# A band buffer's clear moved behind four small GpSimd steps, and three one-input VectorE steps made two-input ones

## The chip, the cores and the metric

The kernel runs on one core of a Trainium2 chip. The metric is the device time of one execution in microseconds (us). The compute engines are TensorE (PE), VectorE (DVE), ScalarE (ACT) and GpSimd (POOL); SyncE (SP) issues most of the DMAs.

## The reference

Two unrelated layers on 2048 tokens of width 448, their outputs side by side:

```python
# A: attention over a dilated window: 16 heads of 28, each token sees itself and 7 tokens at distance 2, 4, .. 14
qkv = x @ wqkv
logits = einsum("bhsd,bhswd->bhsw", q, kg) * scale      # kg, vg: k and v gathered at pos - 2*w, masked below 0
o = einsum("bhsw,bhswd->bhsd", softmax(logits), vg)
a = o.reshape(B, S, D) @ wo
# B: a diagonal complex state space (S5)
dt = exp(log_dt); Lam_bar = exp(dt * Lam)
B_bar = ((Lam_bar - 1) / Lam)[:, None] * Bmat
h[t] = Lam_bar * h[t-1] + B_bar @ x[t]                   # a recurrence over 2048 tokens
y = 2 * real(Cmat @ h) + x * Dskip
return concatenate([a, y], -1)                           # bf16, 1 x 2048 x 896
```

## The kernel before

Nothing schedules the kernel but a string, ORDER. Each of its words names a small function (an "op") with digits for its arguments, a PSUM bank behind "@" and an engine for evictions ("." is ScalarE, "=" is VectorE). The words are worked off once, from left to right, and each engine then runs its own instructions in that order; semaphores alone tie the engines together. So a word that is moved changes the order only on the engines that it uses.

**Attention.** Tokens are transposed on TensorE (XI, XA, XH; their evictions are xi, xa, xh) or by DMA, q and k are made in 64-row blocks (QA, QS, QK) and evicted (qk, qh). The logits are products on VectorE (P, L417, one for each pair of window positions, 24 on 128x2048), summed over each head's rows by TensorE (E_, L429 and L433). They are brought to ScalarE (lt), transposed by DMA (TD, L451), and go through a softmax (sma, smb, smc; sma begins at L457). The weights are then laid out as a band: AL spreads them with matmuls, al evicts them into a buffer Ak (its first two parts are one tile, Ak0, which must be zero outside the band), ad writes Ak to DRAM and sp reads it back on a slant into PT, whose clears on GpSimd are L985. AV and W_ finish the attention.

**The state space.** 2048 steps are done in blocks of T = 4 with rotations. Before that, the parameters of the 448 states, held as 128 partitions by G = 7 columns, are worked out by small ops:

- PP, pcopy, pa, pb, pc bring in the parameters and their exponentials (VectorE and ScalarE). pb leaves f8, each state's angle for 2T tokens as a fraction of a turn.
- pe (VectorE, L639 to L642) makes u4, the angles for five distances, 128x35, and takes off the nearest whole number by adding and subtracting MAGIC = 1.5 * 2^23.
- pf (ScalarE, L646 to L648) takes sine and cosine of u4.
- pd_ (VectorE, L633 to L635) does the same rounding for f8, which gives fT; "way" is a column of -1 and 1.
- tk (L692 on ScalarE, L694 on VectorE), ty, tf and ts make tables of angles for 256 blocks from fT.
- pg (VectorE, L654 to L664) makes co, the correction factors for one to four tokens, and the columns c1t and c2t; rb (L715) spreads co into rotation matrices R.
- ab (GpSimd, L853, four instructions on 64x14) makes from co the columns acol and bcol, which are read by hp much later.

Two more words matter: mz clears Ak0 on GpSimd (L683), and OZ closes the first pools and clears a strip of Z3 on GpSimd (L961). B's input xnB is transposed by DMA into xbuf (xt, L746), which BU multiplies; L899 (xd) multiplies xnB with Dskip.

At the start, GpSimd makes constants (cols, kph, iota, masks), the last of which is shf. The column cols[:, 5:6] holds MAGIC. Around the parameters stand, in ORDER: `pe WF4 pf pd_ tk1= QA01 tk0. QA00 qk000. QA10 QS30 XH1 xh1. XA10 xa10. QA11`. QA11's last matmul (L386) reads what xh1 (a copy of 64x512 on ScalarE) evicts from XH1's bank (L339); its first three are L385.

The loads of all inputs stand first on SP's queue and run to some 30 us; most are issued without a wait for a compute engine.

Of the kernel before, what the change touches and what calls it, by code (L numbers as in the profile page):

```python
# [11 lines left out]
ALU = mybir.AluOpType  # L12
# [8 lines left out]
G = 7  # L21
# [6 lines left out]
MAGIC = 12582912.0  # L28
# [4 lines left out]
WU@0 XI0@1 xi00. LC PP@2 pcopy pa XI2@3 pb xi20. pc WF0 XI1@4 WF1 WF2 xi10= xi01= WF3 xi11= pe WF4 pf pd_ tk1= QA01@5  # L33
tk0. QA00 qk000. QA10@6 QS30@7 XH1@2 xh1. XA10@3 xa10. QA11 XA11@0 xa11. QS20@1 pg rb3 rb0 qk010. wj. QS01@4 ty1
QS11@5 QK041@23 ty0 QK061@06 qk011. QK060 qk001. qk030. qk020. P000 P001 tf0 qh001. qh011. qh000. xt1 ts00 QK040
qk041. QS21@5 QS31@4 P010 P011 P020 qk021. qk031. QK050@71 V_011@03 qk040. qh010. QK051 ts10 V_101@54 qk050. tk4.
E_00@26 P021 E_02 ts20 hc0 P030 E_01 V_010 v011. qk051. V_100 QK100@73 ty4 v010. ty5 P031 P040 tk5. QK101 qk100.
QK111@10 E_03 P041 P050 QK110 qk101. P051 tf2 P060 v100. QK130@73 mz ts02 qk110. v101. tk3. E_04 E_05 qk111. P061 E_06
ts12 tk2. ts22 QK141@51 QK131 qk131. qk130. lt00 QK121@40 QK120 qk120. ty2 BD0 QK140 QK150@37 lt01 TD0 qk121. qk140.
QK161@24 P100 P101 P110 P111 qk141. ci3. QK151 qk151. qk150. V_411@60 P120 P121 P130 ty3 E_10@53 E_12 QK160 qh110.  # L40
P131 P140 V_000@17 qh111. xt3 qh101. qh100. V_410 v410. v411. E_11 P141 P150 xt2 xt0 E_13 V_111@42 V_001 ci2. v000.
sma0 v001. hc1 V_511@60 P151 P160 LD P161 ci0= CD3 V_510 v510. V_500@17 V_110 V_501 tf1 v511. V_401@60 smb0 ci1. ab
E_14 smc0 E_15 E_16 lt10 lt11 v501. v110. tk6. CD2 v111. V_400 v401. dk. TD1 BU100@53 BU000@74 xd2 v400. CD0 BU001 BD1
CD1 BU101 BU111@20 AL1@6 sma1 OZ OP pm3 z00. z10. al1. ad1 AL0@7 BR01 BR11 z11= v500. al0. BU200@56 BU110 smb1 BR12
z01= ts01 smc1 BU301@17 BU201 BU011@34 BU010 z20= BU300 z12. z30= ts11 BR02 BR13 ca3 cs3 BR21 BU500@25 z02= BU501 ca6
ca1 xd0 z13. z21. BU211@13 BR03 z03. z50. BU210 BR22 ts21 xd1 UP1 y1. ad0 BR31 pm0 cs1 AL2@6 wo sp0 z22= UP0 y0. cs6
BR51 BR23 z51. pm1 sa0 BU400@21 pm4 z23. UP2 al2. sp1 AL3@0 AX@4 y2= BU310@56 BU311 z31. BU401 BU511@73 ca2 ca4 sb0
BR32 z32. BU510 ax= adx ad2 al3. BR33 sd0 DN1@4 BR52 cs4 cs2 DN0@5 dn0 z40. BR41 z33. UP3 y3= pm2 ad3 z52. sp2 ca5 dn1
sa2 z41. ty6 BU600@02 tf3 BR53 z53. BU411@75 BU601 AV000@6 AV030@4 av030. H_00@1 BU410 sb2 z60. BR61 h00 H_01@4 h01
ts03 av000. z61. UP5 y5. BR42 AV001@0 AV010@6 sd2 AV031@1 z42. av010. AV021@2 av021. AV020@3 AV011@4 av020= spx hp010  # L50
BR43 z43. av001. av031= BU610@76 UP4 DN2@2 av011. y4= ts13 ca0 DN3@3 dn3 BU611 BR62 z62. W_11@0 W_20@1 dn2 W_01@4
hp012 sa4 hp020 w20. ts23 sp3 w01. BR63 z63. cs5 sb4 H_03@5 h03 sw0 sd4 w11. W_10@3 W_00@2 H_02@7 ow01 W_21@1 w10.
ow10 hp011 UP6 y6= h02 W_31@4 AV130@5 w00. w21= ow20 ow00 av130. AV111@0 av111. AV100@3 AV120@2 AV110@6 av120. av110=
AV131@5 av131= av100. AV121@7 AV101@0 av121. ow11 ow21 sa6 W_30@1 DN5@2 W_60@6 DN4@3 sw2 av101. dn4 w30= sb6 W_71@7
w31. ow31 W_50@5 hp110 hp121 hp023 dn5 hp021 W_41@0 W_61@4 H_05@3 W_51@1 sd6 cs0 ow30 H_04@2 sw4 w71. hp120 w61= w51=
DN6@7 ow71 dn6 w50. C33@5 hy0 ow50 ow61 H_06@4 h05 w41. hp013 hz0 h04 ow41 ow51 C31@0 hp022 hp122 h06 hp111 hy1 hp124
hp025 sw6 hp115 hp112 C30@1 c30 hy2 c31 C32@7 c32 hp015 oc31 hp125 hy5 hp123 C03@3 hz1 W_40@2 hp024 hp113 hz5 hp014
W_70@4 hp114 hp016 hp126 oc30 hz2 hp026 hy4 hy3 hz4 hp116 hz3 hy6 oc32 hz6 w60. w40. w70. xd3 ow70 ow60 C00@1 c33
C01@0 c00 c01 C02@7 c02 C13@6 C11@2 C10@4 oc33 C12@5 c03 c10 c11 oc01 C21@1 C20@0 oc00 ow40 C22@7 CH0@3 oc10 oc03 oc02
CH1@4 c12 oc12 c13 c20 oc13 oc11 c21 c22 ch0 oc20 oc21 oc22 oh0 ch1 oh1  # L60
"""

@with_exitstack
def kernel(
# [17 lines left out]
    V = nc.vector  # L82
# [111 lines left out]
    cols = const.tile([128, 6], F32, tag="cols")  # L194
    hpib, phi, sg, way = (cols[:, i:i + 1] for i in range(4))
# [402 lines left out]
    def small(name, *shape):  # L598
        return const.tile([128, *shape], F32, tag=name, name=name)
    P3 = small("P3", 3, G)  # L600
    lre, lim, ld = (P3[:, i] for i in range(3))
    f8, rk, c1t, c2t, co, fT = (small(*a) for a in (("f8", G), ("rk", 5, G), ("c1t", G), ("c2t", G), ("co", T, 2, G), ("fT", G)))
    dt, are, km, u4, k4, sc2 = (small(*a) for a in (("dt", G), ("are", G), ("km", G), ("u4", 5, G), ("k4", 5, G), ("sc2", 2, 5, G)))
# [26 lines left out]

    @op
    def pd_():
        V.tensor_scalar(km[:], f8[:], MAGIC, None, ALU.add)  # L633
        V.scalar_tensor_tensor(fT[:], km[:], MAGIC, f8[:], ALU.subtract, ALU.subtract)
        V.tensor_scalar(fT[:], fT[:], way, None, ALU.mult)  # L635

    @op
    def pe():
        V.tensor_tensor(u4[:], f8[:].unsqueeze(1).to_broadcast((128, 5, G)), kph[:, 0], ALU.mult)  # L639
        V.tensor_tensor(u4[:], u4[:], kph[:, 1], ALU.add)  # L640
        V.tensor_scalar(k4[:], u4[:], MAGIC, None, ALU.add)  # L641
        V.scalar_tensor_tensor(u4[:], k4[:], MAGIC, u4[:], ALU.subtract, ALU.subtract)  # L642

    @op
# [383 lines left out]
```

## Time and profile before

| | before |
|---|---|
| median of 3 runs | 125.67 us (125.66 to 125.69) |
| the profiled execution's own time | 125.67 us |
| its span, first to last instruction | 124.0 us |
| granted TensorE clock | 1.00 |
| TensorE busy | 117.2 us, 95% of the span |
| VectorE busy | 114.0 us, 92% |
| ScalarE busy | 103.8 us, 84% |
| GpSimd busy | 22.7 us, 18% |

How to read it: a row of a timeline gives the start, the duration, the engine, the line, the operation, what is written and read with shapes, how many such instructions follow each other, and in brackets how long the engine sat idle before and who ended that. The chain that ended last is followed back from the last instruction, at each step to what released it; its rows give start, duration and what ran. "issue" in it is time in which nothing shown was waited for. The digits are the busy tenths in 40 equal slices of the span.

### The profile page before, as it was taken

The page shows a single profiled execution, that of the slowest core. Times are in us where ns is not written, and L with a number is a line of the kernel's source. Part 1 is how long each engine was busy: PE and PEld are TensorE (multiplying, and loading weights), DVE is VectorE, ACT ScalarE, POOL GpSimd, SP SyncE. Part 2 cuts the span into 40 slices and gives each one's busy share as a digit, 9 for nine tenths or more (in the row PEclk, how much of TensorE's full clock was granted, in tenths as well). Part 3 has the DMA queues.
Part 4 walks back from the last instruction along what each step waited for, and adds up shares of the span by engine and source line. Part 5 has one row for each costly group of instructions (what it writes and reads, how often), then busy time and mean ns, then how long its engine had stood idle before and what let it go on. Part 6 is the DMA issues. An engine that isn't in the chain of part 4 may idle for free.

```text
span 124.0 us, 2908 instructions
## 1 busy us (share of the span) xinstructions
PE 117.2 (95%) x1061; PEld 58.8 (47%) x1071; DVE 114.0 (92%) x207; ACT 103.8 (84%) x202; POOL 22.7 (18%) x49
## 2 busy tenths in 40 slices
PE   6994999999999999999999999999999999999990
PEld 6753343434343443453435544645575555555560
DVE  4398999999999999999999999999999999999771
ACT  0949999999997999999999999999999999960000
POOL 6893000000000000004999900000000000000000
PEclk9999999999999999999999999999999999999999
DMA  3998999899997999489999997999656651203652
GB/s 100 271 274 217 326 200 244 199 179 306 227 260 163 211 190 103 92 172 273 304 188 126 137 235 297 153 119 142 151 169 154 178 149 31 80 12 108 220 178 74
DMA packets 56693, 22.34 MB, mean 180 GB/s; under 512 B 42375, under 2 KB 56135, under 8 KB 56679
## 3 DMA queue, kind: packets, MB, share of 16 engines
q1 hardware_dynamic: 56472, 22.08, 80.8%
q8 instruction: 8, 0.13, 0.5%
q10 hardware_dynamic: 207, 0.07, 0.3%
q14 instruction: 6, 0.05, 0.2%
HBM read 9.86 MB, written 6.37 MB: 131 GB/s over the span
## 4 chain that ended last, share of the span: by engine, by line
PE 91%; DVE 3%; ACT 2%; issue 1%; DVEq 0%
PE ps L258 39%; PE ps L909 16%; PE ps L585 10%; PE ps L429 5%; PE ps L773 4%; PE ps L572 4%; PE ps L373 3%; PE ps L276 2%; DVE k L641 2%; PE ps L839 1%; PE ps L934 1%; PE ps L499 1%; PE ps L433 1%; PE ps L374 1%; PE ps L308 1%
## 5 line engine op out<-in xcount | busy, mean ns | idle before, releaser
L417 DVE TENSOR_TENSOR pr<-qf,kf 128x2048 bf16<-128x2048 bf16 x24 | 27.6, 1218 | 0.0
L258 PE MATMUL ps<-xbuf,BT 128*128 128x512 bf16 (+1 forms) x107 | 23.1, 379 | 0.3
L909 PE MATMUL ps<-Cw,Z 128*128 128x448 bf16 x105 | 20.3, 352 | 0.0
L258 PE MATMUL ps<-xT,wq 128*128 128x512 bf16 (+1 forms) x69 | 15.5, 380 | 0.3 <-issue 0.2
L909 PEld LDWEIGHTS <-Z 128*128 128x128 bf16 x105 | 10.3, 98 | 9.6
L258 PEld LDWEIGHTS <-BT 128*128 128x128 bf16 (+1 forms) x112 | 9.0, 97 | 11.9 <-issue 2.8
L585 PE MATMUL ps<-wo,oT 128*128 128x448 bf16 x64 | 13.4, 353 | 0.0
L258 PE MATMUL ps<-wq,xT 128*128 128x448 bf16 (+1 forms) x64 | 12.0, 353 | 0.0
L114 ACT CAST Z<-ps 128x512 bf16<-128x512 f32 (+1 forms) x25 | 11.7, 516 | 0.1
L985 POOL MEMSET PT<- 128x4320 f32 x3 | 11.0, 3696 | 0.1
L258 PEld LDWEIGHTS <-wq 128*128 128x128 bf16 (+1 forms) x72 | 6.0, 97 | 9.0 <-issue 2.5
L734 ACT ACTIVATE ctmp<-Cw,c2t 64x448 f32<-64x448 bf16 x14 | 9.3, 666 | 0.2
L585 PEld LDWEIGHTS <-oT 128*128 128x128 bf16 x64 | 6.2, 98 | 5.6
L961 POOL MEMSET Z<- 128x14 bf16 x1 | 0.1, 111 | 45.3 <-DMA BT<-Bn 45.3
L258 PEld LDWEIGHTS <-xT 128*128 128x128 bf16 (+1 forms) x64 | 5.1, 97 | 6.5 <-issue 1.9
L114 ACT CAST v_s<-ps 128x448 bf16<-128x448 f32 x16 | 8.1, 544 | 0.0
L114 ACT CAST oT<-ps 128x512 bf16<-128x512 f32 x13 | 7.1, 616 | 0.1
L773 PE MATMUL ps<-Z,R 128*128 128x512 bf16 x20 | 6.9, 381 | 0.0
L114 ACT CAST kf<-ps 128x512 bf16<-128x512 f32 x12 | 6.9, 594 | 0.0
L114 ACT CAST ya<-ps 128x448 bf16<-128x448 f32 (+1 forms) x13 | 6.8, 565 | 0.0
L114 ACT CAST qf<-ps 128x512 bf16<-128x512 f32 x12 | 6.7, 607 | 0.0
L429 PE MATMUL ps<-pr,E 128*32 128x512 bf16 x96 | 6.3, 382 | 0.0
(177 smaller groups left out, 231.5 us busy)
## 6 DMA issues: line engine op xcount, KB each, us to landing
PT<-pd SPq DMA_DIRECT2D x16, 156.0 KB, 4.9
out_dram<-ya SPq DMA_DIRECT2D x16, 112.0 KB, 2.4
out_dram<-xbuf SPq DMA_DIRECT2D x15, 112.0 KB, 1.7
pd<-Ak SPq DMA_DIRECT2D x2, 640.0 KB, 3.2
xbuf<-in_A_x_dram SPq DMA_DIRECT2D x2, 448.0 KB, 4.1
xnB<-in_B_x_dram SPq DMA_DIRECT2D x4, 224.0 KB
xnB<-in_B_x_dram SPq DMA_DIRECT2D x4, 192.0 KB, 4.5
PT<-Z SPq DMA_DIRECT2D x6, 128.0 KB, 2.4
```

Of the source, the lines that this page charges most:

```text
L114: (ACT.copy if e == "A" else V.tensor_copy)(o, i)
L258: PE.matmul(o, l, r, start=(first and i == 0), stop=(not first and i == len(pairs) - 1 and not more[s]))
L276: PE.matmul(p[:, 0:128], wz[:], wz[:], start=True, stop=True)
L373: PE.matmul(p[:], wqk(m, slice(0, 128), kt), xT[:, 0, 4 * s + kt], start=(kt == 0), stop=False)
L417: V.tensor_tensor(t[:], q.unsqueeze(1).to_broadcast((128, 4, 512)), k4, ALU.mult)
L429: PE.matmul(acc[s][32 * i:32 * i + 32], E[:, f, ws, :], t[:, i, :], start=(f == 0 and ws == 0), stop=False)
L572: PE.matmul(p[32 * hh:32 * hh + 32, 128 * bl:128 * bl + n], v_s[:, t, 4 * hg + hh, :], PT[:, t % NS, (4 * hg + hh) // HS, (4 * hg + hh) % ...
L585: PE.matmul(p[:, 0:D], late["oT"][:, b // 4, hg, par, 128 * (b % 4):128 * (b % 4) + 128], late["wo"][:, hg, :], start=(hg == 0), stop=(hg ...
L734: ACT.activation(t[a:a + 64, 0:D], Cw[b:b + 64, g, :], ACTF.Copy, scale=c2t[a:a + 64, g:g + 1])
L773: PE.matmul(pp["z", g, j][:], rot(g, 0), late["Z"][:, g, j - 1, :], start=False, stop=True)
L909: PE.matmul(p[:, 0:D], z, Cw[:, g, :], start=(g == 0), stop=(g == G - 1))
L985: POOL.memset(late["PT"][:, 4 * i:4 * i + 4].rearrange("p t g n -> p (t g n)").bitcast(F32), 0.0)
```

## The change

In ORDER, the words ab and mz change places and stand early: `P010 ab mz P011`. Before, mz stood between QK130 and ts02, and ab between ci1 and E_14. On GpSimd, the four instructions of ab now come ahead of the clear of Ak0; nothing else moves on any engine, and SP's queue is the same. In pd_ and pe, three instructions that took a number (MAGIC) or a column (way) as a scalar operand take it as a second input, a column of cols spread over the shape.

```diff
-... QK130@73 mz ts02 ... ci1. ab E_14 ...
+... P010 ab mz P011 ... QK130@73 ts02 ... ci1. E_14 ...
...
     @op
     def pd_():
-        V.tensor_scalar(km[:], f8[:], MAGIC, None, ALU.add)
+        V.tensor_tensor(km[:], f8[:], cols[:, 5:6].to_broadcast((128, G)), ALU.add)
         V.scalar_tensor_tensor(fT[:], km[:], MAGIC, f8[:], ALU.subtract, ALU.subtract)
-        V.tensor_scalar(fT[:], fT[:], way, None, ALU.mult)
+        V.tensor_tensor(fT[:], fT[:], way.to_broadcast((128, G)), ALU.mult)

     @op
     def pe():
         V.tensor_tensor(u4[:], f8[:].unsqueeze(1).to_broadcast((128, 5, G)), kph[:, 0], ALU.mult)
         V.tensor_tensor(u4[:], u4[:], kph[:, 1], ALU.add)
-        V.tensor_scalar(k4[:], u4[:], MAGIC, None, ALU.add)
+        V.tensor_tensor(k4[:], u4[:], cols[:, 5:6].unsqueeze(2).to_broadcast((128, 5, G)), ALU.add)
         V.scalar_tensor_tensor(u4[:], k4[:], MAGIC, u4[:], ALU.subtract, ALU.subtract)
```

More of the change, by code (lines that the diff above doesn't have):

```diff
@@ L35 @@
 QS11@5 QK041@23 ty0 QK061@06 qk011. QK060 qk001. qk030. qk020. P000 P001 tf0 qh001. qh011. qh000. xt1 ts00 QK040
-qk041. QS21@5 QS31@4 P010 P011 P020 qk021. qk031. QK050@71 V_011@03 qk040. qh010. QK051 ts10 V_101@54 qk050. tk4.
-E_00@26 P021 E_02 ts20 hc0 P030 E_01 V_010 v011. qk051. V_100 QK100@73 ty4 v010. ty5 P031 P040 tk5. QK101 qk100.
-QK111@10 E_03 P041 P050 QK110 qk101. P051 tf2 P060 v100. QK130@73 mz ts02 qk110. v101. tk3. E_04 E_05 qk111. P061 E_06
+qk041. QS21@5 QS31@4 P010 ab mz P011 P020 qk021. qk031. QK050@71 V_011@03 qk040. qh010. QK051 ts10 V_101@54 qk050.
+tk4. E_00@26 P021 E_02 ts20 hc0 P030 E_01 V_010 v011. qk051. V_100 QK100@73 ty4 v010. ty5 P031 P040 tk5. QK101 qk100.
+QK111@10 E_03 P041 P050 QK110 qk101. P051 tf2 P060 v100. QK130@73 ts02 qk110. v101. tk3. E_04 E_05 qk111. P061 E_06
 ts12 tk2. ts22 QK141@51 QK131 qk131. qk130. lt00 QK121@40 QK120 qk120. ty2 BD0 QK140 QK150@37 lt01 TD0 qk121. qk140.
@@ L41 @@
 P131 P140 V_000@17 qh111. xt3 qh101. qh100. V_410 v410. v411. E_11 P141 P150 xt2 xt0 E_13 V_111@42 V_001 ci2. v000.
[L42 to L60, printed above, removed]
+sma0 v001. hc1 V_511@60 P151 P160 LD P161 ci0= CD3 V_510 v510. V_500@17 V_110 V_501 tf1 v511. V_401@60 smb0 ci1. E_14
@@ new lines @@
+smc0 E_15 E_16 lt10 lt11 v501. v110. tk6. CD2 v111. V_400 v401. dk. TD1 BU100@53 BU000@74 xd2 v400. CD0 BU001 BD1 CD1
+BU101 BU111@20 AL1@6 sma1 OZ OP pm3 z00. z10. al1. ad1 AL0@7 BR01 BR11 z11= v500. al0. BU200@56 BU110 smb1 BR12 z01=
+ts01 smc1 BU301@17 BU201 BU011@34 BU010 z20= BU300 z12. z30= ts11 BR02 BR13 ca3 cs3 BR21 BU500@25 z02= BU501 ca6 ca1
+xd0 z13. z21. BU211@13 BR03 z03. z50. BU210 BR22 ts21 xd1 UP1 y1. ad0 BR31 pm0 cs1 AL2@6 wo sp0 z22= UP0 y0. cs6 BR51
+BR23 z51. pm1 sa0 BU400@21 pm4 z23. UP2 al2. sp1 AL3@0 AX@4 y2= BU310@56 BU311 z31. BU401 BU511@73 ca2 ca4 sb0 BR32
@@ new lines @@
+z32. BU510 ax= adx ad2 al3. BR33 sd0 DN1@4 BR52 cs4 cs2 DN0@5 dn0 z40. BR41 z33. UP3 y3= pm2 ad3 z52. sp2 ca5 dn1 sa2
+z41. ty6 BU600@02 tf3 BR53 z53. BU411@75 BU601 AV000@6 AV030@4 av030. H_00@1 BU410 sb2 z60. BR61 h00 H_01@4 h01 ts03
+av000. z61. UP5 y5. BR42 AV001@0 AV010@6 sd2 AV031@1 z42. av010. AV021@2 av021. AV020@3 AV011@4 av020= spx hp010 BR43
+z43. av001. av031= BU610@76 UP4 DN2@2 av011. y4= ts13 ca0 DN3@3 dn3 BU611 BR62 z62. W_11@0 W_20@1 dn2 W_01@4 hp012 sa4
+hp020 w20. ts23 sp3 w01. BR63 z63. cs5 sb4 H_03@5 h03 sw0 sd4 w11. W_10@3 W_00@2 H_02@7 ow01 W_21@1 w10. ow10 hp011
@@ new lines @@
+UP6 y6= h02 W_31@4 AV130@5 w00. w21= ow20 ow00 av130. AV111@0 av111. AV100@3 AV120@2 AV110@6 av120. av110= AV131@5
+av131= av100. AV121@7 AV101@0 av121. ow11 ow21 sa6 W_30@1 DN5@2 W_60@6 DN4@3 sw2 av101. dn4 w30= sb6 W_71@7 w31. ow31
+W_50@5 hp110 hp121 hp023 dn5 hp021 W_41@0 W_61@4 H_05@3 W_51@1 sd6 cs0 ow30 H_04@2 sw4 w71. hp120 w61= w51= DN6@7 ow71
+dn6 w50. C33@5 hy0 ow50 ow61 H_06@4 h05 w41. hp013 hz0 h04 ow41 ow51 C31@0 hp022 hp122 h06 hp111 hy1 hp124 hp025 sw6
+hp115 hp112 C30@1 c30 hy2 c31 C32@7 c32 hp015 oc31 hp125 hy5 hp123 C03@3 hz1 W_40@2 hp024 hp113 hz5 hp014 W_70@4 hp114
@@ L61 @@
+hp016 hp126 oc30 hz2 hp026 hy4 hy3 hz4 hp116 hz3 hy6 oc32 hz6 w60. w40. w70. xd3 ow70 ow60 C00@1 c33 C01@0 c00 c01
+C02@7 c02 C13@6 C11@2 C10@4 oc33 C12@5 c03 c10 c11 oc01 C21@1 C20@0 oc00 ow40 C22@7 CH0@3 oc10 oc03 oc02 CH1@4 c12
+oc12 c13 c20 oc13 oc11 c21 c22 ch0 oc20 oc21 oc22 oh0 ch1 oh1
 """
```

## The prediction

> **What bounds the kernel now.** I read the page first: the busy digits, then the chain that ended last.
>
> ```profile
> span 124.0 us, 2908 instructions
> ...
> DVE  4398999999999999999999999999999999999771
> ...
> PE ps L258 39%; PE ps L909 16%; PE ps L585 10%; PE ps L429 5%; PE ps L773 4%; PE ps L572 4%; PE ps L373 3%; PE ps L276 2%; DVE k L641 2%; PE ps L839 1%; PE ps L934 1%; PE ps L499 1%; PE ps L433 1%; PE ps L374 1%; PE ps L308 1%
> ```
>
> VectorE is full from the fifth slice to near the end, and the chain is a list of TensorE's lines. In it one line is foreign: L641, a VectorE step on 128x35 numbers, holds 2% of 124.0 us. So I asked for the chain in order of time, over the first 40 us.
>
> ```profile
> 7.00 2.14 DVE k L641
> 9.14 0.02 issue
> 9.16 0.21 DVE u L642
> 9.37 0.02 issue
> 9.39 0.23 ACT sc L646
> ...
> 11.24 0.59 ACT xT L114
> 11.83 0.04 issue
> 11.88 0.27 PE ps L386
> ```
>
> The chain runs through the small steps for the correction factors (VectorE), their sines (ScalarE), then what stands behind the sines in ScalarE's queue (tk0, the eviction qk000, the eviction xh1), and reaches TensorE at L386, which needs xh1. From 11.88 on the chain in that view holds only TensorE rows and issue gaps. Why L641 takes 2.14 us is told by GpSimd's timeline beside VectorE's:
>
> ```profile
> 6.86 2.23 POOL L683 MEMSET Ak<- 128x2560 f32 x1
> 10.72 0.61 POOL L853 TENSOR_SCALAR acol<-co 64x14 f32<-64x14 f32 x2 [1.63 <-DVE ab L655]
> 11.39 0.58 POOL L853 TENSOR_SCALAR bcol<-co 64x14 f32<-64x14 f32 x2
> ```
>
> ```profile
> 6.33 0.23 DVE L639 TENSOR_TENSOR u<-f,kph 128x35 f32<-128x35 f32 x1
> 6.66 0.30 DVE L640 TENSOR_TENSOR u<-u,kph 128x35 f32<-128x35 f32 x1
> 9.27 0.17 DVE L633 TENSOR_SCALAR km<-f 128x7 f32<-128x7 f32 x1
> 9.67 0.23 DVE L635 TENSOR_SCALAR fT<-fT,cols 128x7 f32<-128x7 f32 x1
> 11.54 0.17 DVE L661 TENSOR_TENSOR t<-cr 128x7 f32<-128x7 f32 x1
> 11.96 2.09 DVE L715 TENSOR_TENSOR R<-Is,co 128x896 bf16<-128x896 bf16 x2
> 13.96 2.36 DVE L417 TENSOR_TENSOR pr<-qf,kf 128x2048 bf16<-128x2048 bf16 x2
> ```
>
> The memset of Ak starts at 6.86 and ends at 9.09. L641 starts at 7.00 and ends at 9.14, 0.05 later. Its neighbours L639 and L640, with as many numbers, take 0.23 and 0.30; the other one-input steps (L633, L635), which run when GpSimd is idle, take 0.17 and 0.23 us. So I read L641 as held by the memset, for about 1.9 of its 2.14 us.
>
> **The change, part by part.**
>
> *L641 becomes a two-input step.* Its nearest row is L639: same shape, two inputs, 0.23 us, with the next step starting 0.33 after it (6.33 to 6.66); L640 to L641 is 0.34. L642 then starts at 7.34, not 9.16: 1.82 us earlier. Bounds: if it costs only what the small L661 does, L642 starts at about 7.2. But the sine then meets ScalarE's table load:
>
> ```profile
> 6.23 1.28 ACT L646 ACT_TABLE_LOAD   x1
> ```
>
> That ends at 7.51, so L646 can't start before it, and the most that can be gained here is 9.39 - 7.51 = 1.88. With L642 at 7.34 and L646 0.23 behind it as before, L646 starts at 7.57: 1.82. If the two-input form were held by the memset too, it would not matter, since the memset is no longer there.
>
> *L633 and L635 become two-input steps.* They run between L642 and tk0 (L692 on ScalarE), which needs fT; the three sine steps of ScalarE run at the same time. L661 (two inputs, 128x7) takes 0.17, as L633 does; L639, with five times the numbers, 0.23. So the cost is 0 to 0.06 each, 0.12 at most for both if the sines cover none of it. I take 0, from L661, the row with the same shape.
>
> A rule against these three edits is in the Trainium skill, "VectorE: DVE Perf Modes", section "The perf-mode tier table": on fp32 a one-input step can run at two elements a cycle and a two-input step at one (2048 elements: 1227 against 2293 ns). By that figure 49 elements would cost an estimated 0.03 us more, and the sum would come out at 123.88; the rows L633 and L661, equal at 0.17, show none of it at 7 elements.
>
> *The memset moves behind the four L853 steps.* On GpSimd it is moved past these four and nothing else, and L853 is freed to run as soon as co is there. It issues no DMA, and the order on SP's queue and on the other engines is as it was. L853 starts 1.82 earlier with its input, at 8.90, and ends at 11.97 - 1.82 = 10.15; the memset then runs to 12.38. GpSimd's and Ak's next users:
>
> ```profile
> 57.29 0.11 POOL L961 MEMSET Z<- 128x14 bf16 x1 [45.32 <-DMA BT<-Bn]
> L114 ACT CAST Ak<-ps x2: 627/634/642, 54.8 to 55.7; 128x512 bf16<-128x512 f32 x2
> ```
>
> Both lie over 40 us later, so the wait itself costs nothing. What it can cost is what runs beside it now: L715 (11.96 moves to 10.14) and the first products L417 (13.96 to 12.14), all with two inputs. From below that is 0 (no reason for a gain); from above it is one memset, 2.23. The rows nearest to it are the later memsets of PT, and two-input steps beside and apart from them:
>
> ```profile
> 58.25 7.34 POOL L985 MEMSET PT<- 128x4320 f32 x2
> 53.78 1.09 DVE L899 TENSOR_TENSOR xnB<-xnB,dsk 128x1792 bf16<-128x1792 bf16 x1
> 63.67 2.08 DVE L899 TENSOR_TENSOR xnB<-xnB,dsk 128x1792 bf16<-128x1792 bf16 x2
> ```
>
> Two of L899 wholly or nearly inside the memset (to 65.59) take 2.08, one outside it 1.09. I take 0.
>
> *What is late next.* ScalarE's steps from L646 to the eviction xh1 all start 1.82 earlier, if what they read is there. xh1 would start at 9.42.
>
> ```profile
> 8.85 0.40 PE L339 MATMUL ps<-ident,xbuf 128*128 128x128 bf16 x4
> 9.53 0.49 PE L385 MATMUL ps<-xT,wq 128*128 128x256 bf16 x3
> 11.88 0.27 PE L386 MATMUL ps<-xT,wzz 128*128 128x256 bf16 x1 [1.85 <-ACT xT L114]
> ```
>
> L339 writes its bank by 9.25, so xh1 isn't held. TensorE's own work ahead of L386 ends at 10.02; L386 could start at 11.88 - 1.82 = 10.06. The idle 1.85 shrinks to some 0.03, and nothing of the 1.82 is lost there.
>
> From there all three compute engines would be 1.82 early, but loads don't move. The loads that could then be late:
>
> ```profile
> DMA packets 166, 0.15 MB, mean 149 GB/s; under 512 B 0, under 2 KB 166, under 8 KB 166
> 25.54 1.46 PE L258 MATMUL ps<-xT,wq 128*128 128x512 bf16 x5
> 36.73 1.25 SPq L451 DMA_TRANSPOSE attn<-lt  x1
> 38.09 5.85 SPq L746 DMA_TRANSPOSE xbuf<-xnB  x3
> xbuf<-xnB SPq DMA_TRANSPOSE x4, 4.4
> 43.56 0.28 DVE L457 TENSOR_TENSOR attn<-attn,mk 128x256 bf16<-128x256 bf16 x1
> L258 PE MATMUL ps<-xbuf,BT x107: 376/379/390, 50.7 to 82.7; 128*128 128x512 bf16 x79, 64*128 64x512 bf16 x28
> ```
>
> The first line is the DMA view of 22 to 23 us: no small packet is left, so the transposes into xT (small packets) have landed by 22.0; their first reader moves from 25.54 to 23.72. The transpose of the logits, issued at 36.73, lands by 41.1 if it takes the 4.4 of the next kind; L457 moves from 43.56 to 41.74. The last of L746's three is issued before 43.94 and should land by 48.3; its reader moves from 50.7 to 48.9. So each has 0.6 to 1.7 us left.
>
> **Sum.** The profiled execution took 125.67 us, which is the median too, with 1.7 around its span of 124.0. Less 1.82: span 122.2, time **123.85**. A difference of 0.2% (0.25 us) is about what a measurement of this kernel can tell from none.
>
> **Rivals.**
>
> A, the gain is partly lost further on. For: DMA stays where it is, and the slack of 0.6 above rests on 4.4 us from another transfer. Were that landing late by a further 1 us, VectorE would lose 0.4, and TensorE behind it at most as much; two such places give 0.8. Time 123.85 + 0.4 = 124.25 or 123.85 + 0.8 = 124.65, say 124.5. Against: nowhere after 12 us does the chain hold a DMA.
>
> B, no gain: L641 was not held by the memset, but is long for its own sake (say for data from elsewhere), or the start was never binding. Then 125.67 stays. Against: the ends at 9.09 and 9.14, and ScalarE and TensorE both idle behind it.
>
> C, slower: a memset holds two-input steps as it held L641. It would then hold L715 or the first L417. VectorE would get 1.82 back at L641 and lose up to 2.23 at 10.15: 0.4 late at its first product. From there it is full for the rest of the kernel and the attention matmuls need the products. Time 125.67 + 0.41 = 126.1; it decides when over 1.82 of the 2.23 falls on VectorE. Against: the L899 rows.
> The Trainium skill, "SBUF — State Buffer", section "Who interferes with whom", speaks against C as well: a two-input VectorE step contends with a GpSimd instruction that reads SBUF, not with one that only writes. By that rule the memset costs nothing; the trace agrees (2.08 for two of L899).
> C's chance is small for the rows' sake.
>
> **How the numbers follow.** The forecast, all engines early by 1.70 (1.82 less 0.12) to 1.88: 0.75 (123.79 to 123.97; a further 0.15 to either side for transfers that fall differently is my choice, a quarter of the margin that the tightest load has: 123.6 to 124.1). A: 0.15. B: 0.04. C: 0.06. The range takes the forecast and A: 123.6 to 124.7; B and C, 0.10 together, lie outside, and the rest of the 2 in 10 is for what my cases miss. Faster by over 0.2%: forecast and A, 0.90; same: B, 0.04; slower: C, 0.06.
>
> **What would show it.** Right: L641 at about 0.25 us, L646 starting near 7.6, L386 near 10.1 with almost no idle before it; the memset of Ak at about 10.1 to 12.4, L715 still 2.09 for two, L417 still 1.18 each; L457 and the first L258 on xbuf 1.8 earlier. Wrong: an L715 or L417 over 2 us (C); a new wait on a DMA between 12 and 51 us (A); L641 still at 2 us (B).

## The result and the profile after

The changed kernel takes 124.12 us (median of 13; 123.70 to 125.28), the kernel before 125.66 (median of 13) beside it: ratio 0.988 (95%: 0.985 to 0.992). Its profiled execution took 123.70. The forecast was 123.85, with rival A (part of the gain lost further on) at 124.25 to 124.65. A few executions of before, and of kernels that keep its stall, run some 1.6 us longer at a granted clock of about 0.98; no reading below rests on them.

One thing differs in kind. Before repeats itself: 12 of its 13 times lie between 125.63 and 125.69. Of the changed kernel's 13, five lie below 123.98 and seven above 124.1. So there are two questions: does the stall at L641 go as told, and where do up to 1.6 us go in some executions?

The page of after:

```profile
span 122.0 us, 2918 instructions
...
DVE  4389999999999999999999999999999999999771
...
PE ps L258 40%; PE ps L909 16%; PE ps L585 10%; PE ps L429 5%; DMA xbuf<-in_A_x_dram 4%; PE ps L773 4%; PE ps L572 4%; PE ps L373 3%; PE ps L839 1%; PE ps L934 1%; PE ps L499 1%; PE ps L433 1%; PE ps L374 1%; SPq L131 1%; PE ps L826 1%; PE ps L785 1%
```

L641 has left the chain, and a load of A's input x has come in with 4%. The chain in order of time leads back to this load (start, duration, what ran):

```profile
2.89 5.47 DMA xbuf<-in_A_x_dram
...
8.41 0.40 PE ps L339 x4
8.80 0.46 PE ps L325 x8
...
9.29 0.59 ACT xT L114
...
9.92 0.27 PE ps L386
```

Neither the small VectorE steps nor the sines are in it any more: the x load lands at 8.36, XH1 (L339) follows, then XA10 (L325), the eviction xh1 at 9.29, and L386. But the step from L325 to xh1 is a near tie. What xh1 reads was written by L339 at 8.81, and ScalarE was busy to 9.26 with the eviction ahead of xh1 (qk000), one step behind the other from the sines on (its rows below). So in this execution ScalarE's queue behind L641 still sets the start of xh1, and the load has some 0.45 us in hand. The timelines of the four compute engines, for the steps of the prediction (VectorE, GpSimd, ScalarE, TensorE):

```profile
6.99 0.20 DVE L641 TENSOR_TENSOR k<-u,cols 128x35 f32<-128x35 f32 x1
7.22 0.20 DVE L642 SCALAR_TENSOR_TENSOR u<-k,u 128x35 f32<-128x35 f32 x1
7.33 0.16 DVE L633 TENSOR_TENSOR km<-f,cols 128x7 f32<-128x7 f32 x1
7.72 0.17 DVE L635 TENSOR_TENSOR fT<-fT,cols 128x7 f32<-128x7 f32 x1
9.94 2.09 DVE L715 TENSOR_TENSOR R<-Is,co 128x896 bf16<-128x896 bf16 x2
11.98 2.36 DVE L417 TENSOR_TENSOR pr<-qf,kf 128x2048 bf16<-128x2048 bf16 x2
```

```profile
8.70 0.61 POOL L853 TENSOR_SCALAR acol<-co 64x14 f32<-64x14 f32 x2 [1.79 <-DVE ab L655]
9.89 2.23 POOL L683 MEMSET Ak<- 128x2560 f32 x1
```

```profile
6.14 1.28 ACT L646 ACT_TABLE_LOAD   x1
7.45 0.23 ACT L646 ACTIVATE sc<-u 128x35 f32<-128x35 f32 x1
...
8.67 0.59 ACT L114 CAST qf<-ps 128x512 bf16<-128x512 f32 x1
9.29 2.10 ACT L114 COPY xT<-ps 64x512 bf16<-64x512 bf16 x3
```

```profile
9.92 0.27 PE L386 MATMUL ps<-xT,wzz 128*128 128x256 bf16 x1 [0.34 <-ACT xT L114]
48.73 3.51 PE L258 MATMUL ps<-xbuf,BT 128*128 128x512 bf16 x18
```

L641 takes 0.20 instead of 2.14. The memset (9.89 to 12.12) runs beside L715 and the first L417, which take 2.09 and 2.36 for two as before. L386 starts 1.96 earlier, the first L258 on xbuf 1.96 earlier (48.73 against 50.69), and the execution is 1.97 shorter.

### The profile page after: what moved, and what is told of

Read it like the earlier page. It is cut to its first block, busy times and chain, and to the rows that moved or that the text cites. A ratio compares the mean times of both kernels' runs of the same rounds, so it can differ in the third digit from the quotient of the medians.

```text
span 122.0 us, 2918 instructions
## 1 busy us (share of the span) xinstructions
PE 117.3 (96%) x1071; PEld 59.0 (48%) x1071; DVE 112.3 (92%) x207; ACT 103.9 (85%) x202; POOL 22.6 (19%) x49
## 4 chain that ended last, share of the span: by engine, by line
PE 90%; DMA 4%; SPq 2%; ACT 0%; DVE 0%; issue 0%
PE ps L258 40%; PE ps L909 16%; PE ps L585 10%; PE ps L429 5%; DMA xbuf<-in_A_x_dram 4%; PE ps L773 4%; PE ps L572 4%; PE ps L373 3%; PE ps L839 1%; PE ps L934 1%; PE ps L499 1%; PE ps L433 1%; PE ps L374 1%; SPq L131 1%; PE ps L826 1%; PE ps L785 1%
## 5 line engine op out<-in xcount | busy, mean ns | idle before, releaser
L417 DVE TENSOR_TENSOR pr<-qf,kf 128x2048 bf16<-128x2048 bf16 x24 | 27.6, 1219 | 0.0
L258 PE MATMUL ps<-xbuf,BT 128*128 128x512 bf16 (+1 forms) x112 | 23.7, 379 | 0.0
L258 PE MATMUL ps<-xT,wq 128*128 128x512 bf16 (+1 forms) x72 | 15.8, 380 | 0.0
L258 PEld LDWEIGHTS <-BT 128*128 128x128 bf16 (+1 forms) x112 | 9.0, 97 | 11.9 <-issue 2.8
L258 PE MATMUL ps<-wq,xT 128*128 128x448 bf16 (+1 forms) x64 | 12.0, 353 | 0.0
L258 PEld LDWEIGHTS <-wq 128*128 128x128 bf16 (+1 forms) x72 | 6.0, 97 | 9.0 <-issue 2.5
L258 PEld LDWEIGHTS <-xT 128*128 128x128 bf16 (+1 forms) x64 | 5.1, 97 | 6.5 <-issue 1.9
```

The lines of the kernel that those rows point to most:

```text
L258: PE.matmul(o, l, r, start=(first and i == 0), stop=(not first and i == len(pairs) - 1 and not more[s]))
L417: V.tensor_tensor(t[:], q.unsqueeze(1).to_broadcast((128, 4, 512)), k4, ALU.mult)
```

## The experiments

### 1 and 2: each half alone

The first takes only the new ORDER (ab and mz), the second only the three two-input steps, both on the kernel before.

```diff
 first:
-... QK130@73 mz ts02 ... ci1. ab E_14 ...
+... P010 ab mz P011 ... QK130@73 ts02 ... ci1. E_14 ...
 second (and L633, L635 likewise):
-        V.tensor_scalar(k4[:], u4[:], MAGIC, None, ALU.add)
+        V.tensor_tensor(k4[:], u4[:], cols[:, 5:6].unsqueeze(2).to_broadcast((128, 5, G)), ALU.add)
```

> Only the words ab and mz are moved; L633, L635 and L641 stay one-input steps. Theory (the clear alone held L641): L641 at 0.17 to 0.25 us, the clear at about 10 to 12.3, the time that of the changed kernel, 123.7 to 124.4, with its spread. Rival 1 (one-input steps are long for their own sake): L641 stays near 2.1 us and the time near 125.66. Rival 2 (the form is what matters, the place is not): as rival 1.

> Only L633, L635 and L641 become two-input steps; the clear of Ak0 keeps its place ahead of ab and runs at 6.9 to 9.1. Theory (a clear, which only writes, holds one-input fp32 steps and not two-input ones): L641 at 0.2 to 0.3 us beside the clear, the time that of the changed kernel, 123.7 to 124.4; ab starts at about 9.1, behind the clear, instead of 8.7, which nobody waits for. Rival (a clear holds two-input steps too): L641 at about 2.1 us and 125.66.

Measured: the move alone 124.87 us (124.45 to 125.76; ratio 0.994, 0.990 to 0.997), two inputs alone 124.83 (124.01 to 126.07; 0.990, 0.986 to 0.995). Both medians lie above the 123.7 to 124.4 that I expected. VectorE's and GpSimd's timelines, first of the move alone, then of two inputs alone:

```profile
7.34 0.18 DVE L641 TENSOR_SCALAR k<-u 128x35 f32<-128x35 f32 x1
10.30 2.23 POOL L683 MEMSET Ak<- 128x2560 f32 x1
```

```profile
7.01 0.20 DVE L641 TENSOR_TENSOR k<-u,cols 128x35 f32<-128x35 f32 x1
6.88 2.23 POOL L683 MEMSET Ak<- 128x2560 f32 x1
```

The same one-input L641 takes 0.18 with no memset beside it; with two inputs it takes 0.20 while the memset (6.88 to 9.11) runs. So it was the pair, one-input step beside the memset, that cost 1.9 us, and either half removes it. The Trainium skill, "SBUF — State Buffer", section "Who interferes with whom", has it so: one-input steps in a two-port mode exclude GpSimd, a two-input step contends only with a GpSimd instruction that reads. The trace agrees, with 2.14 against 0.20 beside the same memset; in which mode L641 ran no trace shows.

### 3 and 4: the changed kernel again, to see what differs

> The changed kernel once more, for another profiled execution: its times lay between 123.7 and 125.28 where before lay within 0.06. Theory (early loads land at other times in each execution, and the 2 us at L641 had covered it): in an execution that takes over 124.2, an engine waits longer for the x load of L156 (L339 later than 9.0) or for a transpose into xT. Rival (the engines' own races, such as ab beside pg, differ): L339 as in the first profile, and a VectorE or GpSimd row is longer.

> As the one before it: a further profiled execution of the changed kernel, to see one of the longer ones. Same expectations.

Two profiled executions of the unchanged kernel after: 125.03 and 124.76 us, both at clock 1.00. L641 is short in both. The first differs at the start and at 50 us; its waits in the first 13 us (engine and line, what was waited for, us in total, times, longest):

```profile
PEld L385 <- DMA wq<-in_A_wqkv_dram: 0.7, 2, 0.4
...
DVE pr L417 <- ACT kf L114: 0.6, 1, 0.6
ACT xT L114 <- PE ps L339: 0.6, 1, 0.6
PEld L339 <- DMA xbuf<-in_A_x_dram: 0.5, 1, 0.5
```

Its timelines of TensorE and VectorE:

```profile
9.50 0.40 PE L339 MATMUL ps<-ident,xbuf 128*128 128x128 bf16 x4
12.63 2.36 DVE L417 TENSOR_TENSOR pr<-qf,kf 128x2048 bf16<-128x2048 bf16 x2 [0.57 <-ACT kf L114]
50.09 3.50 PE L258 MATMUL ps<-xbuf,BT 128*128 128x512 bf16 x17 [0.33 <-ACT v_s L114]
```

L339 has to wait for its loads and runs at 9.50 instead of 8.41; so ScalarE waits 0.6 for xh1, and VectorE 0.6 at its first product, 0.65 later than in the first profile of after. This is a wait that the stall at L641 would have covered: in before L339 ran at 8.85 and L386 not until 11.88.

Number 4 doesn't show the sign that I had named: its L339 runs at 8.76, not later than 9.0. Its 0.30 us at the first product are there at L641 already, which starts at 7.29 instead of 6.99; ahead of it VectorE waits 0.59 us for the transposes of L308, which it did not in the first profile of after.

At 50 us, TensorE has an idle gap that the first profile of after has not. The timeline puts it down to an eviction of v_s. But in the first profile of after the same matmul runs at 48.73, while that eviction (from 48.69 on) is still under way. What holds TensorE is a wait for the DMA transposes of B's input. Ahead of this matmul its queue has two semaphore waits of its own at L258; here they are (duration in ns, min/median/max, then first and last start), in the first profile of after and in number 3:

```profile
L258 PEldq EVENT_SEMAPHORE  x2: 51/86/120, 47.2 to 47.4; - x2
```

```profile
L258 PEldq EVENT_SEMAPHORE  x2: 51/1018/1985, 47.9 to 50.0; - x2
```

In number 3 the long one runs from 47.94 to 49.92, and the last landing of L746 is at 49.89. In every profile with a gap this wait ends 0.03 to 0.04 behind that landing, and the matmul starts 0.2 to 0.3 behind it. The table gathers all profiles of kernels with a short L641 and the DMAs unchanged; landings are from the trace's semaphore records. (The execution in the last row is the longest of that kernel's ten, at a clock of 1.00.)

| profile | L339 | first L417 | L746's last issues start | last landing | idle before L258 on xbuf | its start | that less 48.73 | time less 123.70 |
|---|---|---|---|---|---|---|---|---|
| after | 8.41 | 11.98 | 38.50 | 47.31 | 0 | 48.73 | 0 | 0 |
| move alone | 9.60 | 12.73 | 39.77 | 48.48 | 0 | 49.73 | 1.00 | 0.99 |
| after, 4 | 8.76 | 12.28 | 39.57 | 49.59 | 0.36 | 49.79 | 1.06 | 1.06 |
| after, 3 | 9.50 | 12.63 | 39.88 | 49.89 | 0.33 | 50.09 | 1.36 | 1.33 |
| after, 9 (below) | 9.50 | 12.63 | 40.13 | 50.00 | 0.44 | 50.20 | 1.47 | 1.46 |
| two inputs alone | 9.46 | 12.59 | 40.28 | 50.83 | 1.05 | 51.12 | 2.39 | 2.37 |

The last two columns agree to 0.03: all that an execution loses against 123.70 it has lost by the first L258 on xbuf. The move alone has no gap there; of its 1.00, 0.75 stands at the first product and 0.25 comes between. In the other rows the gap comes on top: number 3 loses 0.65 by the first product and 0.33 at the gap, number 4 0.30 and 0.36, number 9 0.65 and 0.44, two inputs alone 0.61 and 1.05. That is not the whole: another 0.38 to 0.73 us of each of these four losses comes between, and I have not followed it.

The traces also show that the loads did move. In before and in number 5 below, which keeps the stall, L746's last issues start at 38.09 and 38.13 and the last landing is at 46.42 and 46.45. In every row of the table both are later, though the compute engines are ahead. From its first issue at L167 to the first load of Bn, SyncE takes 11.4 and 12.0 us in these two profiles, and 12.4 to 13.0 in all nine profiles here without the stall. Part of that is the six loads of L177, first in before, then in the first profile of after:

```profile
11.08 3.07 SPq L177 DMA_DIRECT2D xnB<-in_B_x_dram  x6
```

```profile
10.63 4.26 SPq L177 DMA_DIRECT2D xnB<-in_B_x_dram  x6
```

They take 3.07 and 3.40 us with the stall and 3.67 to 4.57 without it. Why is not shown.

### 5: the clear cut in two

If GpSimd's hold ended with each of its instructions, L641 would get in after half of the clear. On the kernel before:

```diff
-        POOL.memset(Ak0.rearrange("p k n -> p (k n)").bitcast(F32), 0.0)
+        for k in range(2):
+            POOL.memset(Ak0[:, k].bitcast(F32), 0.0)
```

> The kernel before, with the clear of Ak0 at its old place cut into two memsets of 128x1280 f32 (1.1 us each); L641 is a one-input step as before. Theory (the hold is of one GpSimd instruction at a time, and whoever asks first gets the next turn): L641 waits for the first half only and takes about 1.1 us instead of 2.13; the time is 125.66 less 1.0, 124.6, or more in executions where loads are late; the spread is smaller than that of the changed kernel, since 0.9 us of cover is left. Rival (GpSimd's next instruction keeps the hold, or the hold is for the whole queue): L641 stays at 2.1 us, 125.66. Second rival (VectorE asks in the gap and both halves are late): L641 at 1.1, the clear's second half starts 0.2 later; same time as the theory.

Measured: 125.71 us, ratio 1.000 (0.996 to 1.004): no gain. GpSimd and VectorE (the clear's line is one lower here):

```profile
6.85 2.27 POOL L684 MEMSET Ak<- 128x1280 f32 x2
6.99 2.17 DVE L641 TENSOR_SCALAR k<-u 128x35 f32<-128x35 f32 x1
```

My theory of turns by instruction fell: L641 ends at 9.16, 0.04 behind the second memset. The Trainium skill, in the section named above, gives the shared ports to whoever issues first, for the whole instruction; here a step that stood waiting from 6.99 was passed over by the second memset too. In the trace the second starts at 7.96, before the first has ended (8.02), so there was no gap between them. The run disagrees with that reading, unless two memsets back to back count as one; what it is inside GpSimd stays open.

### 6 and 7: fewer transfers ahead of the late ones

If the last transposes of L746 are late because the DMA engines are busy, taking work from ahead of them should close the gap. Groups 4 to 6 of B's matrix (Bn), and the transposes that need groups 2 and 3, are issued behind them; number 6 does this on the changed kernel, number 7 on the kernel before, where the stall still stands.

```diff
+    Bn_load(0, D, 0, 0, 4)
+    Bn_load(D, 512, 384, 0, G)
...
-        gs = slice(4 * i, 4 + 3 * i)
+        gs = (slice(0, 2), slice(4, G), slice(2, 4))[i]
+        if i == 2:
+            Bn_load(0, D, 0, 4, G)
...
-... xt2 xt0 E_13 ...
+... xt2 xt0 BD2 E_13 ...
```

> The changed kernel with less DMA work ahead of the last transpose of B's input (L746): the loads of Bn for the last three of seven groups, and the transposes into BT for groups 2 and 3, are issued behind it instead of ahead; nothing is left out. Theory (the spread of 123.7 to 125.3 comes from DMA: early x and weight loads, 0 to 0.75 us, and this last transpose landing at 47.3 to 50.8 where TensorE wants it at 48.7): the transpose lands 2 to 3 us earlier, TensorE's wait for it near 49 to 51 us is gone, and the times fall to 123.6 to 124.6, median about 124.0; what is left comes from the first 10 us. Rival (TensorE's wait near 50 us is for ScalarE's evictions of v, with the transpose only a bystander): times as before the edit, 123.7 to 125.3.

> The same lighter DMA edit on the kernel before, with the clear and the one-input steps as they were: a control. Theory (the stall of 1.9 us at L641 covers the late landings): no change, 125.66 with a spread under 0.1. Rival (the DMA edit is a gain of its own): below 125.5.

Measured: on the changed kernel 124.03 us (five of six between 123.74 and 124.14, and of these the ratio: 0.984, 0.979 to 0.989; the sixth, 125.62, has no profile and stays unexplained), on the kernel before 125.47 (ratio 0.9985, 0.993 to 1.004; seven of its ten times 125.45 to 125.50). TensorE and SyncE in number 6 (L261 is L258, L751 is L746):

```profile
36.75 5.84 SPq L751 DMA_TRANSPOSE xbuf<-xnB  x3
49.30 3.51 PE L261 MATMUL ps<-xbuf,BT 128*128 128x512 bf16 x18
```

The transposes are issued 3.1 earlier than in profile 3, and TensorE has no gap before the matmul; its two semaphore waits there take 0.05 us each. But the control was not still: the same edit makes before 0.2 us faster, which is what its rival said (below 125.5). The ratio's interval includes 1, but those seven times all lie below the lowest of before (125.64). That 0.2 is no part of the gap at 50 us, which before doesn't have. It fits with number 6, whose first L258 on xbuf is 0.57 behind the first profile of after, while its time is only 0.33 behind: the edit gives some 0.2 back later. Where, I have not found out.

### 8, 9 and 10: the early loads, and both side by side

Number 8 takes number 6 and loads x ahead of the first weights for k, with XH1 ahead of QA10 in ORDER. Number 9 is the changed kernel, number 10 the kernel of number 6, on the same chip.

```diff
-    w_load(0, 256, 0, D)
+    w_load(0, 256, 0)
     SP.dma_start(xnA[:, 4:8], xA_r[:, 4:8])
+    w_load(0, 256, D)
...
-... QA10@6 QS30@7 XH1@2 xh1. XA10@3 xa10. QA11 ...
+... XH1@2 xh1. XA10@3 xa10. QA10@6 QS30@7 QA11 ...
```

> The changed kernel with the lighter DMA of the run before, and in addition the load of x's tokens 512 to 1023 (L156) issued ahead of the first k weights instead of behind them, and its transposes (XH1, XA10) ahead of QA10 and QS30 on TensorE; nothing is left out. Theory (what is left of the spread is the landing of this load, which holds the eviction xh1 and through it ScalarE's queue): xh1 starts behind qk000 without a wait for TensorE in every profile, the first product starts at 11.9 to 12.2, and the times lie between 123.5 and 124.0, median about 123.7. Rival (all early loads are late together, so the k weights are then what is late): xh1 is early but ScalarE waits for QA10's result, and the spread stays at 0.4 us or more.

> The changed kernel again, beside the other two on the same chip: 123.7 to 125.3 with a median of about 124.3 if the spread is its own and not that chip's or that hour's.

> The changed kernel with the lighter DMA once more, for more times beside the other two: 123.7 to 124.5, median about 124.0, if TensorE's wait for the last transpose of B's input was the larger part of the spread; the same as the changed kernel if it was not.

Measured, beside 125.67 for before: 

| | us | ratio (95%) |
|---|---|---|
| 8, x first and fewer transfers | 125.09 (124.87 to 126.08) | 0.995 (0.992 to 0.998) |
| 9, the changed kernel | 124.87 (123.98 to 125.46) | 0.993 (0.990 to 0.995) |
| 10, fewer transfers | 123.82 (123.72 to 124.47) | 0.985 (0.981 to 0.990) |

Number 8 did not do what I expected. TensorE, ScalarE and VectorE there (L389 and L390 are L385 and L386, L329 is L325, L421 is L417):

```profile
9.00 0.50 PE L389 MATMUL ps<-xT,wq 128*128 128x256 bf16 x3
10.24 0.27 PE L390 MATMUL ps<-xT,wzz 128*128 128x256 bf16 x1 [0.74 <-ACT xT L114]
...
9.61 1.62 ACT L114 COPY xT<-ps 64x512 bf16<-64x512 bf16 x2
12.07 0.59 ACT L114 COPY xT<-ps 128x512 bf16<-128x512 bf16 x1 [0.84 <-PE ps L329]
13.25 1.23 DVE L421 TENSOR_TENSOR pr<-qf,kf 128x2048 bf16<-128x2048 bf16 x1 [0.89 <-ACT kf L114]
```

xh1 came without a wait for TensorE (9.61), and the weights for k held TensorE little: L389 of QA10 runs at 9.00, behind XA10. What is late is QA10's last matmul, L390. It reads the rows of xT that xh1 writes, and with xh1 ahead of QA10 in ORDER it now waits 0.74 us for it. QS30, QA11 and XA11 (L329 at 11.65) stand behind it on TensorE, and the first product came at 13.25, later than in any other profile without the stall. So number 8 put a wait for ScalarE in the place of one for a load, by its own new ORDER, and neither its theory nor its rival was tested. That a late x load costs 0.6 to 0.75 at the first product in some executions is shown by four profiles (numbers 1, 2, 3 and 9); no run here removed it.

The median of number 9 is above the 124.3 that I expected; the spread is the kernel's own on this chip too. Numbers 9 and 10 are the pair that tells. SyncE's queue in the first profile of after, then in number 9 with its TensorE row:

```profile
7.51 1.35 SPq L145 DMA_DIRECT2D wq<-in_A_wqkv_dram  x2
8.90 1.69 SPq L167 DMA_DIRECT2D xbuf<-in_A_x_dram  x3
...
21.41 0.64 SPq L187 DMA_DIRECT2D Bn<-in_B_B_re_dram  x1
...
38.50 5.87 SPq L746 DMA_TRANSPOSE xbuf<-xnB  x3
```

```profile
7.94 2.00 SPq L145 DMA_DIRECT2D wq<-in_A_wqkv_dram  x2
9.99 1.69 SPq L167 DMA_DIRECT2D xbuf<-in_A_x_dram  x3
...
22.67 0.64 SPq L187 DMA_DIRECT2D Bn<-in_B_B_re_dram  x1
...
40.13 5.88 SPq L746 DMA_TRANSPOSE xbuf<-xnB  x3
...
50.20 3.50 PE L258 MATMUL ps<-xbuf,BT 128*128 128x512 bf16 x17 [0.44 <-ACT v_s L114]
...
DMA to landing us min/median/max: 4.1/5.1/6.1
```

The two losses have a common beginning: the landing of the x load that SyncE issues at 2.89 in both executions. It lands at 8.36 in the first profile of after and at 9.45 in number 9. L339 follows it (8.41 and 9.50), and so does SyncE itself. Its waits between 5 and 11 us (us in total, times, longest), first of after, then of number 9:

```profile
SPq L145 <- DMA xbuf<-in_A_x_dram: 0.4, 1, 0.4
```

```profile
SPq L145 <- DMA xbuf<-in_A_x_dram: 1.0, 1, 1.0
```

So the instructions up to the last of the weights (L145) take SyncE until 9.94 instead of 8.86. The queue is then 1.09 late at L167, 1.26 at the loads of Bn and 1.63 at the last transposes; these take up to 6.1 us to land, and TensorE stands 0.44 us. With fewer transfers (10):

```profile
36.88 5.87 SPq L751 DMA_TRANSPOSE xbuf<-xnB  x3
...
49.05 3.51 PE L261 MATMUL ps<-xbuf,BT 128*128 128x512 bf16 x17
```

The transposes start 3.25 earlier than in 9, and TensorE has no gap, as in number 6. The median falls by 1.05 us, though the time of 10 still varies (123.72 to 124.47). Of this drop 0.2 is the edit's own by number 7, and 0.44 the gap as profile 9 shows it. Some 0.4 is left; profile 10 has its first product at 12.14, 0.49 before that of 9, but the edit first changes the queue at 22 us and can't be the cause of that, so I leave this part open. This version has the lowest median of the three on this chip, with the ratios above.

## Why the prediction was right, and where it was not

**L641 held by the memset: right.** Predicted a step of about 0.25 us, measured 0.20; L646 at 7.45 against 7.57. It is earlier by 1.94, not 1.82. I called 1.88 the most because of the table load; that began 0.09 earlier too (6.14), and ended at 7.42. Numbers 1 and 2 show the hold itself. They show as well that the change does one thing twice, which the prediction said only in passing.

**L633 and L635 at no cost: right.** 0.16 and 0.17 us, against 0.17 and 0.23 with one input.

**The memset beside two-input steps at no cost: right**, rival C is out: L715 and L417 unchanged beside it. Rival B is out with L641 at 0.20.

**L386 with an idle time of 0.03: nearly.** It is 0.34, since L339 ran earlier (8.41, not 8.85) with the x load, and TensorE's work ahead of L386 with it. L386 itself is at 9.92 (10.06 predicted).

**"What is late next": the term that was mis-sized.** I wrote that loads don't move, and that each had 0.6 to 1.7 us left, from one profile and one landing time of 4.4 us. The first profile of after has such a margin (landing 47.31, matmul 48.73, 1.4 us in hand), and the forecast of 123.85 is right for such executions (123.70 to 123.84 in four of the first 13). But the loads became later, and by other amounts from one execution to the next. In before the last of L746 landed at 46.42, earlier than my 48.3. Without the stall it landed anywhere from 47.31 to 50.83, partly for a later issue (the group starts between 38.50 and 40.28, not at 38.09), partly for a longer way (up to 6.3 us in profile 3, at most 4.6 in before). And L339, for which I took 8.85, ran between 8.41 and 9.60. In before there was room for that: TensorE's idle 1.85 ahead of L386 held the start, and the matmul on xbuf came at 50.69, 4.3 behind the landing. A stall that repeats in every execution can cover late loads, and the even times of before said nothing of them. How far its own landings spread, two profiles with the stall (46.42 and 46.45, L339 at 8.85 and 8.51) can't tell.

So rival A, for which I gave 0.15, was the usual case: a loss of 0.42 in the first median (124.12 less 123.70), of 1.17 in the second (124.87). Its mechanism, a DMA that becomes late, was right, its place not: I had VectorE lose at L457; the losses stand at the first product (0.3 to 0.75) and at TensorE's first L258 on xbuf (0.33 to 1.05). In the second set they go beyond A's 0.8 for two places.

The range of 123.6 to 124.7 holds the first median, 124.12, and nine of its 13 times. It doesn't hold the second, 124.87, of the same kernel in number 9, nor the medians of numbers 1 and 2. So that the number came out inside the range is in part luck; the mechanism at L641 is not.

Left open: why the x load, issued at 2.89, lands up to a microsecond later in some executions of one kernel than in others, why SyncE's issues take longer without the stall, where the 0.2 of number 7 comes from, and the 0.4 in the comparison of 9 and 10.

## What to carry to other kernels

Before you count the whole of a removed stall as gain, list the transfers whose landing it covered, and give each the spread that landings show over executions, not the one value of one profile, nor the place that they had beside the stall; times that repeat to 0.05% can be the work of the stall itself. When a kernel becomes faster and less even at once, compare the profiles of two of its executions row by row: the first row whose start differs names the next bound. A small one-input fp32 step on VectorE beside a long clear on GpSimd is worth a look, and one of the two edits is enough.

## What the runs showed of the hardware that was not expected

- Two memsets back to back hold a one-input VectorE step as long as one does: 2.17 us for two halves, 2.14 for one whole.
- The same x load, issued at 2.89, landed at 8.36 us in one execution of a kernel and at 9.45 in another; SyncE waits for it and was done with its first loads at 8.86 and 9.94. The same DMA transposes took at most 4.6 us from issue to landing in before, at most 6.1 in number 9.
- An idle time of TensorE that the timeline put down to an eviction (0.33 to 1.05 us, ACT v_s) was a wait for a DMA: the semaphore wait of its queue at that line ended 0.03 to 0.04 us behind the landing.
